# A fused attention, feed-forward and expert kernel: when the first feed-forward weights are loaded, and in which order the second head pair is prepared

## The chip, the cores and the metric

The kernel runs on one core of a Trainium2 chip. The metric is the device time of one launch in microseconds, lower is better. The kernel before takes 721.33 us (median of three runs, 720.0 to 721.43).

## The reference

Three stages follow each other. Shapes are fixed; all arrays are float32.

```python
# 1 attention within clusters: batch 2, heads 8, seq 768, head_dim 64, 16 clusters per head
q_assign = argmax(q_n @ c_n.T); k_assign = argmax(k_n @ c_n.T)      # normalised rows and centroids
mask   = q_assign[:, :, :, None] == k_assign[:, :, None, :]
scores = where(mask, q @ k.T / sqrt(64), -1e9)
attn   = exp(scores - max) / (sum + 1e-9)
x      = (attn @ v) -> (1536, 512)
# 2 feed-forward: w_in (512, 2048), w_out (2048, 512)
h = x @ w_in;  g = max(h, 0) + alpha * min(h, 0);  x = g @ w_out
# 3 experts: 8 of them, top 1, for tokens with x @ w_skip > 0
e = argmax(x @ w_gate);  x[t] += gate * (relu(x[t] @ w1[e]) @ w2[e])
```

Only stage 1 is touched, together with the conversion of the first three blocks of stage 2's weights, which is spread over stage 1.

## The kernel before

Stage 1 works on eight head pairs, n = 0 to 7. A pair has 12 steps: k = 0 to 5 are the six row tiles of its first head, k = 6 to 11 those of the second, so that step i = 12 n + k. The order of the work is written out by hand: the loop of `attention` runs over the steps, and every engine gets its instructions in the order in which the loop calls the helpers. Nothing is rescheduled afterwards.

**A step.** `scores` (S) multiplies a tile of AB by AB (L305) and adds CD by CD (L308) into a PSUM tile s; DVE takes the row maximum (`highest`, L321), ACT the exponential (`expo`, L328). Two steps later PE transposes it (`transp`, L339), ACT copies the halves to eth (L341) and DVE takes the remainder etl (L342); a group of three steps is then multiplied by v (`pv`). There are two tiles s, so scores of step i+2 wait for `expo` of step i.

**The next pair, m = n + 1, is prepared while pair n runs.** Tp holds its transposed q and k (`load`). `scaleq` scales q on POOL (L225). `sims` multiplies Tp by the centroids on PE (L188, after steps k = 1 and 2), DVE finds maxima, and POOL weighs them (`weigh`, L201). `sims2` makes the one-hot cluster rows oh (on POOL L216, L217). `split` writes RL: the rounded parts of q and k (part 0, L233, four instructions) and their remainders (part 1, L238, four). `onehots` turns oh on PE (L252, tile po), and ACT copies it to st (L263, L264). `place` copies RL into AB and CD of one head (three DMAs, L283 to L285, 384 KB each), `placeoh` copies st into the last rows of CD (three DMAs, L290, 32 KB each). RL has one buffer: the next pair's `split` waits until all `place` copies of this pair have read it. There is one AB and one CD for each of the two heads; the second head's copies are issued at k = 0 of the pair itself.

**At the end of a head pair** POOL also widens the reciprocal sums (`recip`, rx, L388), which PE transposes (`recip2`, pb, L397), and normalises the output of the pair before (L409 to L412, eight instructions of about 1 us).

**The feed-forward weights** come as raw 64-bit words. `Convert.load` fetches a block f (two DMAs of 512 KB, L551 and L552); `steps` converts it in four quarters of four slots each: two instructions on ACT (L579, L580), then one on DVE in each of three slots (L582, L584, L586), and one on POOL (L588) in the slot that opens the next quarter. A slot is used at steps i from CV0 on, except at k in CVX = (5, 6, 7, 8, 11). After a block the block f + 2 is loaded and REST slots stay empty.

**DMAs.** All those named are issued by SP, in program order. Each completion has one of eight semaphores in turn, and an issue waits until the DMA eight before it has landed.

Of the kernel before, what the change touches and what calls it, by code (L numbers as in the profile page):

```python
# [84 lines left out]
XG = (1, 6)  # L85
HT = 4
PACE = 7.5
CV0 = 12
LK = 8
XB = 3  # L90
LATE = 3
# [1 line left out]
PREP = (33, 45)  # L93
OK = 8
CVX = (5, 6, 7, 8, 11)
REST = 4
SIM, SP, S2, VS = (1, 2), (2, 3), 3, (8, 10)
ORD = ("SMAPXaBbE", "SMAPaVBXEb", "SAPXBMabE")

# [1 line left out]
def attention(ctx, tc, A, cst, xs, Tp, conv=None, prepare=None, then=None):  # L101
# [101 lines left out]
    def sims2(n, xs=(0, 1)):  # L203
        eq = pairs[n]
        if xs[0] == 0:
            hots[n] = hk.tile([P, 2, NT, 32], BF16, tag="oh", name="oh", bufs=1)
        g = G // 2
        gs = slice(xs[0] * g, (xs[-1] + 1) * g)
        m2 = wk.tile([P, G], F32, tag="m2", name="m2")
        nc.vector.tensor_reduce(out=m2[:, gs], in_=eq[:, gs], axis=AX.X, op=ALU.max)  # L210
        oh, mb = hots[n].rearrange("p x t (j c) -> p (x t j) c", c=NC_)[:, gs], m2[:, gs].unsqueeze(2).to_broadcast([P, gs.stop - gs.start, NC_])
        if n == 0:
            nc.vector.tensor_tensor(out=oh, in0=eq[:, gs], in1=mb, op=ALU.is_equal)
        else:

            nc.gpsimd.tensor_tensor(out=eq[:, gs], in0=eq[:, gs], in1=mb, op=ALU.subtract)  # L216
            nc.gpsimd.tensor_scalar(out=oh, in0=eq[:, gs], scalar1=-1.0, scalar2=1.0, op0=ALU.max, op1=ALU.add)  # L217
# [9 lines left out]
    def split(n, part):  # L227
        if part == 0:
            RL = wk.tile([P, 4, S], F32R, tag="RL", name="RL", bufs=1)
            heads[n] = RL  # L230
            for x in range(2):
                for u in halves:
                    nc.gpsimd.tensor_tensor(out=RL[:, 1 + x, u], in0=Tp[:, x, u], in1=zero.to_broadcast([P, S // 2]), op=ALU.add)  # L233
        else:
            RL = heads[n]
            for x in range(2):
                for u in halves:
                    nc.gpsimd.tensor_tensor(out=RL[:, 3 * x, u], in0=Tp[:, x, u], in1=RL[:, 1 + x, u].bitcast(F32), op=ALU.subtract)  # L238
# [10 lines left out]
    def turn(oh, po, x):  # L249

        for g in range(2):
            nc.tensor.matmul(po[:96, (2 * x + g) * P:(2 * x + g + 1) * P], lhsT=oh[:, x, 3 * g:3 * g + 3].rearrange("p t c -> p (t c)"),  # L252
                             rhs=identb, start=True, stop=True)

    def onehots(n):
        oh = hots.pop(n)
        po = ps_t.tile([P, 512], F32, tag="pt", name="po")
        for x in range(2):
            turn(oh, po, x)
        pv = po.rearrange("p (x g s) -> p x g s", x=2, g=2)  # L260
        st = hk.tile([96, 2, 2, P], F32R, tag="st", name="st", bufs=1)
        heads[n, "st"] = st
        nc.scalar.copy(st[:, 0], pv[:96, 0])  # L263
        nc.scalar.activation(st[:, 1], pv[:96, 1], AF.Copy, bias=-BIG, scale=BIG)  # L264
# [22 lines left out]
    def placeoh(n, j):  # L287
        o = slice(D + j * NC_, D + (j + 1) * NC_)
        for t in range(3):
            nc.sync.dma_start(out=CDs[j][o].bitcast(F32).rearrange("p x (g t s) -> p x g t s", g=2, t=3)[:, :, :, t],  # L290
                              in_=heads[n, "st"][32 * t + j * NC_:32 * t + (j + 1) * NC_].bitcast(F32))
# [6 lines left out]
    def scores(i):  # L298
        hd, t = divmod(i, NT)
        n, j = divmod(hd, 2)  # L300
        AB, CD = ABs[j], CDs[j]
        s = ps_s.tile([P, 2, 512], F32, tag="s", name="s")
        for u in range(2):
            ks = slice(u * 384, (u + 1) * 384)
            nc.tensor.matmul(s[:, u, :384], lhsT=AB[:, 0, t * P:(t + 1) * P], rhs=AB[:, 1, ks], start=True, stop=False)  # L305
        for u in range(2):
            ks = slice(u * 384, (u + 1) * 384)
            nc.tensor.matmul(s[:, u, :384], lhsT=CD[:, 0, t * P:(t + 1) * P], rhs=CD[:, 1, ks], start=False, stop=True)  # L308
        if t % 3 == 0:
            if j == 0:  # L310
                dens[n, t // 3] = wk.tile([P, 2, 3], F32, tag="den", name="den", bufs=4)
            den = dens[n, t // 3][:, j]
            eth = wk.tile([P, NT, 384], F32R, tag="eth", name="eth", bufs=2)
            etl = wk.tile([P, NT, 384], F32R, tag="etl", name="etl", bufs=2)
            grp[i // 3] = (den, eth, etl)
        es[i] = s
# [65 lines left out]
    def recip(n, g):  # L382
        rd = wk.tile([P, 2, 3], F32, tag="rd", name="rd")
        nc.vector.tensor_scalar(out=rd, in0=dens[n, g], scalar1=1e-9, scalar2=None, op0=ALU.add)
        nc.vector.reciprocal(out=rd, in_=rd)
        rx = wk.tile([P, 3, 2, D], F32, tag="rx", name="rx", bufs=1)
        eng = nc.gpsimd if n < len(seq) - 1 else nc.vector
        eng.tensor_copy(rx.rearrange("p t j d -> p j t d"), rd.unsqueeze(3).to_broadcast([P, 2, 3, D]))  # L388
        dens[n, g] = rx
# [55 lines left out]
    def before():  # L445
        for f in range(3):
            yield from conv.steps(f, 4)
            if f < 2:
                conv.load(f + 2)
                for _ in range(REST):  # L450
                    yield
# [3 lines left out]
    for i in range(NI + L + 7):  # L455
        n, k = divmod(i, 12)
        m = n + 1
        if i == NI and then is not None:
            early.close()
            for _ in first:  # L460
                pass
            fill = then()
            next(fill)
        if conv is not None and i in (2, 3):
            conv.load(i - 2)
        if conv is not None and i == PREP[0]:
            nc.sync.dma_start(out=al, in_=A["alpha"].rearrange("(f p) -> f p", p=P))
        if conv is not None and i == PREP[1]:
            pa = ps_t.tile([P, 512], F32, tag="pt", name="pa")
            nc.tensor.transpose(pa[:, :DFF // P], al, ident[:DFF // P, :DFF // P])  # L470
            prepare(pa[:, :DFF // P])
        if i % 3 == 1 and 0 <= i - 4 < NI and (i - 4) // 3 % 4 > 1:
            recip((i - 4) // 12, (i - 4) // 3 % 2)
        gi, part = divmod(i - L - 3, 3)
        live = 0 <= gi < NI // 3
        back = 0 <= i - L < NI
        for do in ORD[i % 3]:
            if do == "S" and i < NI:
                scores(i)
            if do == "S" and k == 0 and n < len(seq):  # L480
                place(n, 1)
                placeoh(n, 1)
            if do == "M" and i < NI:
                highest(i)
            if do == "P" and live:
                pv(gi, part)
                if part == 1 and gi % 4 > 1:
                    recip2(gi // 4, gi % 2)
            if do in "AB" and back:
                transp(i - L, "AB".index(do))  # L490
            if do in "ab" and back:
                lows["ab".index(do)]()
            if do == "V" and live:
                evac(gi)
            if do == "E" and i < NI:
                expo(i)
            if do == "X" and conv is not None and CV0 <= i and (k not in CVX or i >= NI - 12):

                next(first, None)
        if live and part == 2 and gi % 4 > 1:  # L500
            late.append((i + (LATE if i < NI else 0), gi))
        if late and late[0][0] <= i:
            gl = late.pop(0)[1]
            spare += normalize(gl // 4, gl % 2)
            while spare and i < NI:
                spare.pop(0)()
        for _ in range(FILL[max(i - NI, 0)] if i >= NI else 0):
            next(fill, None)
            if spare and i > NI + NRM:
                spare.pop(0)()  # L510
        if m < len(seq):
            if k in SIM:
                sims(m, SIM.index(k))
            if k == S2 and m == 1:
                sims2(m)
            if k in SP:
                split(m, SP.index(k))
            if k == S2 and m > 1:
                sims2(m)
            if k == 6:  # L520
                place(m, 0)
            if k == (OK if m > 1 else OK - 1):
                onehots(m)
                placeoh(m, 0)
            if k == LK and m + 1 < len(seq):
                load(m + 1)
            if k == VS[0]:
                vsplit(m, 0)
            if k == VS[1]:
                vsplit(m, 1)  # L530
            if k == 11 and m + 1 < len(seq):
                scaleq(m + 1)
# [1287 lines left out]
```

## Time and profile before

| | |
|---|---|
| median of 3 runs | 721.33 us |
| the profiled execution: time, span of the profile | 721.68 us, 719.9 us |
| PE, DVE, ACT, POOL busy, of the span | 97%, 79%, 66%, 53% |
| chain that ended last: PE, DMA, DVE, POOL, ACT | 67%, 9%, 6%, 6%, 5% |
| TensorE clock granted, mean | 0.994 |

The profiled execution is 0.35 us above the median. The span holds everything between the first and the last instruction; 1.8 us lie around it. Busy time of PE is that of pipelined matmuls, whose ends are modelled, so that short gaps of PE are read from the starts of its instructions. Stage 1 lies between about 13 us and 250 us.

### The profile page before, as it was taken

How to read it: one execution, taken by the hardware profiler on the slowest of the kernel's cores; microseconds unless marked ns; L12 is line 12 of the kernel's file. 1: busy time of each engine (PE TensorE's matmuls, PEld its weight loads, DVE VectorE, ACT ScalarE, POOL GpSimd, SP SyncE). 2: the span in 40 equal slices, each digit the busy share in tenths (PEclk: the TensorE clock that was granted, in tenths of full speed). 3: DMA queues.
4: the chain of work that ended last, by engine and by line, in shares of the span. 5: the costliest groups of instructions: out<-in, count | busy, mean ns of one | idle time of the engine just before them, and what ended most of it. 6: DMA issues, size and time to landing. Idle time of an engine off the chain costs nothing.

```text
span 719.9 us, 11791 instructions
## 1 busy us (share of the span) xinstructions
PE 701.3 (97%) x4119; PEld 627.2 (87%) x4119; DVE 566.4 (79%) x1112; ACT 471.9 (66%) x904; POOL 382.3 (53%) x339
## 2 busy tenths in 40 slices
PE   8999999999999999999999999999999999999995
PEld 5989999989998899888889999999888989898884
DVE  5888998799989878888884989977468888786651
ACT  5779798888889964445544655556645867574640
POOL 4539797697976486666662000001025888884201
PEclk9999999999999999999999999999999999999998
DMA  7885678656775133334303600016443998997000
GB/s 208 212 198 128 148 171 180 160 138 140 169 179 104 61 117 117 117 127 136 132 16 117 192 0 1 1 59 198 151 150 130 385 381 312 346 348 268 33 10 25
DMA packets 44128, 109.21 MB, mean 152 GB/s; under 512 B 8730, under 2 KB 24554, under 8 KB 38688
## 3 DMA queue, kind: packets, MB, share of 16 engines
q1 hardware_dynamic: 36992, 67.81, 34.6%
q0 software_dynamic: 7072, 40.60, 15.2%
q8 instruction: 34, 0.56, 0.3%
q14 instruction: 30, 0.25, 0.1%
HBM read 74.78 MB, written 10.10 MB: 118 GB/s over the span
## 4 chain that ended last, share of the span: by engine, by line
PE 67%; DMA 9%; DVE 6%; POOL 6%; ACT 5%; issue 4%; SPq 1%; POOLq 0%; ACTq 0%; DVEq 0%
PE h L671 18%; PE y L720 15%; DMA raw<-in_wall_dram,wi 6%; PE yo L1204 5%; PE pt L339 4%; PE hw L1257 4%; PE h L1204 3%; PE s L305 2%; PE px L357 2%; PE s L308 2%; PE y L730 2%; ACT e L328 2%; PE sim L188 2%; PE px L359 2%; DVE etl L342 2%
## 5 line engine op out<-in xcount | busy, mean ns | idle before, releaser
L342 DVE TENSOR_TENSOR etl<-pt,eth 128x384 fp32r<-128x384 f32 x192 | 102.1, 549 | 20.4 <-ACT eth L341 19.1
L341 ACT CAST eth<-pt 128x384 fp32r<-128x384 f32 x192 | 91.1, 486 | 21.7 <-PE pt L339 21.7
L1171 POOL DMA_INDIRECT xg<-y1d,gi x16 | 27.6, 1727 | 130.1 <-DVE gi L1020 113.8
L339 PE MATMUL pt<-ident,e 128*128 128x128 f32 x576 | 94.5, 274 | 0.3 <-ACT e L328 0.3
L321 DVE TENSOR_REDUCE nm<-s 128x1 f32<-128x768 f32 x96 | 90.4, 943 | 3.9 <-PE s L308 3.7
L328 ACT ACTIVATE e<-s,nm 128x768 f32<-128x768 f32 x96 | 87.4, 911 | 4.2 <-DVE nm L321 3.3
L699 ACT CAST gh<-gm 128x384 fp32r<-128x384 f32 x60 | 30.9, 514 | 81.7 <-DVE gm L697 58.5
L339 PEld LDWEIGHTS pt<-ident,e 128*128 128x128 f32 x576 | 74.2, 141 | 7.1 <-ACT e L328 0.6
L701 DVE TENSOR_TENSOR gl<-gm,gh 128x384 fp32r<-128x384 f32 x60 | 49.4, 823 | 25.7 <-ACT gh L699 25.7
L357 PE MATMUL px<-etl,vh 128*64 128x384 f32 (+1 forms) x192 | 65.4, 368 | 1.4 <-DVE etl L342 1.1
L305 PE MATMUL s<-AB 128*128 128x384 f32 x192 | 57.6, 381 | 2.3 <-ACT e L328 2.0
L571 POOL TENSOR_TENSOR pre<-ct,pre 128x512 int32<-128x512 int32 x26 | 37.2, 1452 | 35.8 <-DVE ct L569 35.8
L671 PE MATMUL h<-xh,wh 128*128 128x384 f32 x256 | 55.6, 338 | 0.6 <-DVE gm L694 0.4
L671 PE MATMUL h<-xh,wl 128*128 128x384 f32 x256 | 56.0, 339 | 0.0
L671 PE MATMUL h<-xl,wh 128*128 128x384 f32 x256 | 55.0, 336 | 0.0
L1539 DVE TENSOR_TENSOR wl<-raw,wh 128x2048 fp32r<-128x2048 f32 (+2 forms) x26 | 44.4, 1713 | 12.3 <-ACT wh L1535 11.0
L359 PE MATMUL px<-eth,vh 128*128 128x384 f32 x160 | 54.0, 337 | 0.0
L308 PE MATMUL s<-CD 128*128 128x384 f32 x192 | 49.7, 340 | 1.5 <-DMA CD<-st 1.0
L671 PEld LDWEIGHTS h<-xh,wh 128*128 128x128 f32 x256 | 45.5, 188 | 3.3 <-DVE gm L694 0.5
L671 PEld LDWEIGHTS h<-xh,wl 128*128 128x128 f32 x256 | 44.6, 188 | 2.7 <-POOL wl L643 2.6
L671 PEld LDWEIGHTS h<-xl,wh 128*128 128x128 f32 x256 | 45.7, 188 | 0.0
L1535 ACT CAST wh<-raw 128x2048 fp32r<-128x2048 f32 (+2 forms) x26 | 37.3, 1443 | 11.2 <-PE yo L1204 11.2
(352 smaller groups left out, 1815.3 us busy)
## 6 DMA issues: line engine op xcount, KB each, us to landing
AB<-RL SPq DMA_DIRECT2D x32, 384.0 KB, 5.2
raw<-in_w_in_dram SPq DMA_DIRECT2D x16, 512.0 KB, 4.0
raw<-in_w_out_dram SPq DMA_DIRECT2D x16, 512.0 KB, 4.7
raw<-in_wall_dram SPq DMA_DIRECT2D x8, 1024.0 KB, 7.4
Tp<-in_qkT_dram SPq DMA_DIRECT2D x16, 384.0 KB, 3.7
CD<-RL SPq DMA_DIRECT2D x16, 384.0 KB, 6.8
raw<-in_wall_dram POOLq DMA_DIRECT2D x4, 1024.0 KB
vt<-in_v_dram SPq DMA_DIRECT2D x8, 384.0 KB, 6.2
```

The lines of the kernel that those rows point to most:

```text
L305: nc.tensor.matmul(s[:, u, :384], lhsT=AB[:, 0, t * P:(t + 1) * P], rhs=AB[:, 1, ks], start=True, stop=False)
L308: nc.tensor.matmul(s[:, u, :384], lhsT=CD[:, 0, t * P:(t + 1) * P], rhs=CD[:, 1, ks], start=False, stop=True)
L321: nc.vector.tensor_reduce(out=nm, in_=s[:, :, :384], axis=AX.XY, op=ALU.max, negate=True)
L328: nc.scalar.activation(e.rearrange("p (u c) -> p u c", u=2), s[:, :, :384], AF.Exp, bias=nm, accum_out=den[:, i % 3:i % 3 + 1])
L339: nc.tensor.transpose(pt[:, i2], e[:, kt * P:(kt + 1) * P], ident)
L341: nc.scalar.copy(eh, pt)
L342: lows[u] = lambda: nc.vector.tensor_tensor(out=etl[:, 3 * u:3 * u + 3, q * P:(q + 1) * P], in0=pt, in1=eh.bitcast(F32), op=ALU.subtract)
L357: nc.tensor.matmul(px[:m], lhsT=vh[:, kt, :m], rhs=etl[:, kt], start=False, stop=False)
L359: nc.tensor.matmul(px, lhsT=vh[:, kt, :], rhs=eth[:, kt], start=False, stop=(kt == NT - 1))
L671: nc.tensor.matmul(hs[c], lhsT=a[:, k * P:(k + 1) * P], rhs=x[:, k, c * HC:(c + 1) * HC], start=(k == 0 and i == 0), stop=(k == KD - 1 and ...
L720: nc.tensor.matmul(ys[gi * GT + t], lhsT=a[:, t * P:(t + 1) * P], rhs=w, start=(f == 0 and n == 0), stop=(gi == 0 and f == NF - 1 and n == 2))
L1204: nc.tensor.matmul(out, lhsT=l[:, k], rhs=r[:, k * DM:(k + 1) * DM], start=start and k == 0 and i == 0, stop=stop and k == 3 and i == len( ...
```

## The change

Three things are moved; no instruction is added or removed.

- The raw blocks 0 and 1 are loaded at steps 9 and 21 instead of 2 and 3 (RAW).
- The conversion's first slot is step 16 instead of 12 (CV0), and two slots instead of four stay empty after a block (REST).
- For the second pair (m = 1) both parts of `split` follow `sims2` at k = 3, where part 0 stood ahead of it at k = 2; and `onehots` with `placeoh` follows step 6 and stands ahead of `place`, where it followed step 7 and stood behind `place`.

```diff
+RAW = (9, 21)
-CV0 = 12
+CV0 = 16
-REST = 4
+REST = 2
...
-        if conv is not None and i in (2, 3):
-            conv.load(i - 2)
+        if conv is not None and i in RAW:
+            conv.load(RAW.index(i))
...
             if k == S2 and m == 1:
                 sims2(m)
-            if k in SP:
+                split(m, 0)
+                split(m, 1)
+            if k in SP and m > 1:
                 split(m, SP.index(k))
             if k == S2 and m > 1:
                 sims2(m)
+            if k == (OK if m > 1 else 6):
+                onehots(m)
+                placeoh(m, 0)
             if k == 6:
                 place(m, 0)
-            if k == (OK if m > 1 else OK - 1):
-                onehots(m)
-                placeoh(m, 0)
```

SP's queue, from the raw loads to the copies for the second head of the second pair, before (AB0, CD0: first head, AB1, CD1: second head):

```order
L551 DMA raw0_78<-in_w_in_dram 128x4x256
L552 DMA raw0_78<-in_w_out_dram 128x1024
L283 DMA AB0_165<-RL_341 64x1536
L285 DMA CD0_166<-RL_341 64x2x768
L290 DMA CD0_166<-st_492 16x4x128 x3
L130 DMA Tp_91<-in_qkT_dram 128x768 x2
L132 DMA vt_526<-in_v_dram 128x2x384
L283 DMA AB1_167<-RL_341 64x1536
L285 DMA CD1_168<-RL_341 64x2x768
```

The same stretch of SP's queue now (line numbers are 1 to 3 higher in the changed file):

```order
L291 DMA CD0_166<-st_456 16x4x128 x3
L284 DMA AB0_165<-RL_368 64x1536
L286 DMA CD0_166<-RL_368 64x2x768
L131 DMA Tp_91<-in_qkT_dram 128x768 x2
L133 DMA vt_522<-in_v_dram 128x2x384
L554 DMA raw0_78<-in_w_in_dram 128x4x256
L555 DMA raw0_78<-in_w_out_dram 128x1024
L284 DMA AB1_167<-RL_368 64x1536
L286 DMA CD1_168<-RL_368 64x2x768
```

The one-hot copies now lead the RL copies of the first head, and the raw load of block 0 stands between the third pair's loads and the copies for the second head. Block 1 takes the same place one pair later.

POOL's queue in the second pair's preparation, before:

```order
L233 TENSOR_TENSOR RL<-Tp,zero 128x384 x4
L216 TENSOR_TENSOR eq<-eq,m_373 128x384
L217 TENSOR_SCALAR oh<-eq 128x384
L238 TENSOR_TENSOR RL<-Tp,RL 128x384 x4
L246 TENSOR_TENSOR vh<-vt,vh 128x6x64
```

And now:

```order
L217 TENSOR_TENSOR eq<-eq,m_364 128x384
L218 TENSOR_SCALAR oh<-eq 128x384
L234 TENSOR_TENSOR RL<-Tp,zero 128x384 x4
L239 TENSOR_TENSOR RL<-Tp,RL 128x384 x4
L247 TENSOR_TENSOR vh<-vt,vh 128x6x64
```

The one-hots moved ahead of the four casts. One pair later, POOL's queue behind the one-hots of the third pair was before:

```order
L217 TENSOR_SCALAR oh<-eq 128x384
L588 TENSOR_TENSOR w32a<-raw_78,w32a 128x256
L409 TENSOR_TENSOR xa<-xa,xb 128x384
L410 TENSOR_TENSOR xa<-xa,rb 128x384
L411 TENSOR_TENSOR xh_86<-xa,zero 128x384
```

And is now:

```order
L218 TENSOR_SCALAR oh<-eq 128x384
L410 TENSOR_TENSOR xa<-xa,xb 128x384
L411 TENSOR_TENSOR xa<-xa,rb 128x384
L412 TENSOR_TENSOR xh_86<-xa,zero 128x384
L413 TENSOR_TENSOR xl_87<-xa,xh_86 128x384
```

The conversion's L588 (L591 in the changed file) left this place, since the conversion opens a quarter later.

## Rows read from the trace of the kernel before

**Rows 1.** Windows, third pair: stretch, us, busy time and count by engine, clock, DMA.

```profile
73.86:103.50 29.64, 29.11 (x206) 27.25 (x204) 26.65 (x51) 26.13 (x63) 25.06 (x28) 1.00 0.65 147
```

**Rows 2.** Timeline of PE: start us, us, engine, line, op, tiles, idle before and releaser.

```profile
42.12 0.59 PE L308 MATMUL s<-CD 128*128 128x384 f32 x2 [0.99 <-DMA CD<-st]
...
64.48 0.39 PE L252 MATMUL po<-identb,oh 128*96 128x128 bf16 x4
...
72.77 0.34 PE L359 MATMUL px<-eth,vh 128*128 128x384 f32 x1
73.23 0.55 PE L397 MATMUL pb<-ident,rx 128*128 128x128 f32 x3
```

**Rows 3.** Timeline of SP's queue: first the copies of pair 1's first head.

```profile
29.37 0.52 SPq L283 DMA_DIRECT2D AB<-RL  x1
...
35.69 0.59 SPq L285 DMA_DIRECT2D CD<-RL  x1
...
37.03 3.44 SPq L290 DMA_DIRECT2D CD<-st  x3
...
44.10 1.91 SPq L285 DMA_DIRECT2D CD<-RL  x1
```

**Rows 4.** Line L283, the issue at 29.37: us from issue to landing.

```profile
DMA to landing us min/median/max: 3.8/3.8/3.8
```

**Rows 5.** Line L285, the issue at 44.10: us from issue to landing.

```profile
DMA to landing us min/median/max: 8.9/8.9/8.9
```

**Rows 6.** Line L290, three issues from 66.6 on: duration ns; us to landing.

```profile
L290 SPq DMA_DIRECT2D CD<-st x3: 586/622/637, 66.6 to 68.0; - x3
...
DMA to landing us min/median/max: 2.0/2.0/2.0
```

**Rows 7.** Line L551, raw loads issued at 21.39 and 23.74: us to landing.

```profile
DMA to landing us min/median/max: 6.0/6.3/6.5
```

**Rows 8.** Line L552, raw loads issued at 22.02 and 24.21: us to landing.

```profile
DMA to landing us min/median/max: 6.8/7.1/7.3
```

**Rows 9.** Timeline of ACT around steps 6 and 7 of the first pair.

```profile
30.63 0.91 ACT L328 ACTIVATE e<-s,nm 128x768 f32<-128x768 f32 x1
...
32.73 0.92 ACT L328 ACTIVATE e<-s,nm 128x768 f32<-128x768 f32 x1
...
33.87 0.40 ACT L264 ACTIVATE st<-po 96x256 fp32r<-96x256 f32 x1
```

**Rows 10.** Timeline of POOL, from the second pair's preparation on.

```profile
26.16 3.18 POOL L233 TENSOR_TENSOR RL<-Tp,zero 128x384 fp32r<-128x384 f32 x4 [1.74 <-DMA CD<-st]
...
31.75 3.92 POOL L238 TENSOR_TENSOR RL<-Tp,RL 128x384 fp32r<-128x384 f32 x4
...
52.21 1.01 POOL L201 TENSOR_TENSOR eq<-eq,cw 128x384 f32<-128x384 f32 x1 [4.90 <-DMA CD<-st]
53.17 3.37 POOL L233 TENSOR_TENSOR RL<-Tp,zero 128x384 fp32r<-128x384 f32 x4
...
61.31 1.50 POOL L217 TENSOR_SCALAR oh<-eq 128x384 bf16<-128x384 f32 x1
62.79 0.75 POOL L588 TENSOR_TENSOR w32a<-raw,w32a 128x256 int32<-128x256 int32 x1
...
72.67 0.50 POOL L388 COPY rx<-rd 128x384 f32<-128x384 f32 x1
```

**Rows 11.** Waits of PE from 73 to 225 us: us in total, times, longest.

```profile
PE s L305 <- ACT e L328: 1.7, 5, 0.5
PE px L357 <- DVE etl L342: 0.8, 2, 0.6
```

**Rows 12.** Timeline of POOL, the same casts one pair later and in pair 4.

```profile
82.74 3.23 POOL L233 TENSOR_TENSOR RL<-Tp,zero 128x384 fp32r<-128x384 f32 x4
...
141.91 3.19 POOL L233 TENSOR_TENSOR RL<-Tp,zero 128x384 fp32r<-128x384 f32 x4
```

**Rows 13.** Line L285, the issue at 72.20 (second head of pair 2): us to landing.

```profile
DMA to landing us min/median/max: 9.0/9.0/9.0
```

## The prediction, on record before the result was known

> **What bounds the kernel now.** I read the page first: PE is busy for 97% of the span, so only gaps of PE count in stage 1. Next the windows: a pair of heads takes 29.64 us, of which PE shows 29.11 us, and the other engines 25 to 27 us each [rows 1]. Little can be won, but POOL, at 25.06 us, has hardly more room than PE, and what it does in a pair is one chain. Then PE's rows at the second pair: it idles 0.99 us at the first scores, at 42.12, until the last copy of st into CD has landed, and about 0.3 us at 73.23, where the transpose of rx comes 0.46 us behind the matmul at 72.77, while such matmuls there follow each other at 0.17 [rows 2]. The second gap is POOL's: from 52.21 on it has no idle time before the rx of 72.67 [rows 10]. From 73 us to 225 us PE waits 1.7 us for exponentials and 0.8 us for etl [rows 11]; what the spacing of the conversion costs is in these.
>
> **Part 1, the one-hots first.** Their price is counted from the copies into AB and CD that step 12 needs. POOL's idle 1.74 us at 26.16 lets the one-hots run ahead of the casts; the work is the same, so the remainders L238 end no later than before, at 31.75 + 3.92 = 35.67 us [rows 10]. St is made one step earlier: it ended at 33.87 + 0.40 = 34.27, and the exponentials ahead of it stand at 30.63 and 32.73, so it is ready near 32.2 [rows 9]. ACT still does the same in these steps, and PE's two transposes change places with a step of equal work: nothing. The three issues take 0.6 us each and land in 2.0 us when the queue is empty [rows 6], so they are done near 34.3, and only then come the RL copies, which had begun at 29.37 [rows 3]. One alone takes 3.8 us [rows 4]; against 2.0 us for the small ones that leaves about 1.8 us of transfer for 384 KB. The three therefore land near 34.3 + 3.8 = 38.1, 39.9 and 41.7 us. Before, the last landing was just short of 42.12 [rows 2], near 41.9. So the wait of 0.99 us doesn't go: its cause passes from the small copies to the large ones, and I count 0.2 us gained. Bounds: 1.0 us gained (the wait gone) to 1.0 us lost (each copy 0.3 us slower and the transfers of the next pair, issued right behind, in their way).
>
> The Trainium skill (DMA: Bandwidth & Descriptors, Anatomy of one DMA) gives 2.0 us fixed and the bytes at 436 GB/s, fitted to the other issue path. By it a 384 KB copy would take 2.9 us, the three would land by about 38.5, and the wait would be gone. The 3.8 us row speaks against that, since it was alone in the queue.
>
> **Part 2, block 0 loaded at step 9.** Before, the raw loads landed at 21.39 + 6.0 = 27.4, 28.8, 30.3 and 24.21 + 7.3 = 31.5 us [rows 7, 8], while SP had nothing else to copy until 29.37 [rows 3]; the first RL copy landed in its lone 3.8 us [rows 4]. They cost nothing there, so moving them gains nothing there. A block holds the queue for two of these intervals, 2 x (31.5 - 27.4) / 3 = 2.7 us. At step 9 it stands behind the next pair's loads and in front of the copies for the second head. Their last one landed at 44.10 + 8.9 = 53.0 us [rows 3, 5], and POOL's casts for the third pair, which overwrite the RL that it reads, began at 53.17, just as POOL was free of L201 [rows 10]. That was a cover of 0.2 us. Now the copy lands near 53.0 - 0.2 + 2.7 = 55.5, and the casts start near 55.6, 2.4 us late. Scores of the second head have time to spare; POOL has not. The one-hots of the third pair end at 61.31 + 1.50 + 2.4 = 65.2, and PE wants to turn them at 64.48 [rows 2, 10]: 0.7 us of the delay shows there. The conversion's L588 of 0.75 us at 62.79 has left this stretch, so rx is 2.4 - 0.75 = 1.65 us late, and so is the transpose at 73.23, which already waited for it. Pair 1 loses 1.65 us in all. Bounds: 0.3 us gained (loads that don't hold up the copies, and L588 gone) to 3.2 us lost (a block that takes 4.2 us, half as long again as these).
>
> **Part 3, block 1 at step 21.** Its copy landed at 72.20 + 9.0 = 81.2, and the casts began at 82.74 behind L201 [rows 12, 13]: 1.5 us of cover. PE and L201 are 1.65 us later now, while the copies, which follow the one-hots, are only 0.7 us later plus 2.7 for the block, at 84.6. The casts would start at 82.74 + 1.65 = 84.4. Cost 0.2 us, counted as nothing; without the cover it would be 2.7 us.
>
> **Part 4, the conversion.** Up to step 37 the slots have the same kind of work in both, for the shift of four steps is one quarter; the last quarter of block 0 falls on steps 38 to 45, which were empty. Block 1 follows with fewer empty slots. The two ACT instructions that open a quarter move from steps 12, 46, 51, 60, 64 to 38, 49, 57, 62, 70. Steps k = 0 to 2 have room on ACT, since PE does sims there; at the others they delay an exponential, which PE sees two steps later. Of such places three go (46, 51, 64) and two come (57, 70). Of the waits of 1.7 and 0.8 us at most half hangs on these, and POOL, which now has an L588 more in pair 3, gives part of it back. I take 0.5 us gained; bounds 2.5 us gained (all of these waits) and 0.75 us lost (that L588 alone, shown in full).
>
> **The sum.** -0.2 + 1.65 - 0.5 = +0.95 us. On the profiled execution's 721.68 us, of which 719.9 us are the span, that is 722.6; the profiled execution stood 0.35 us above the median of the runs, so the median comes to 722.3 us. What a measurement can tell from no change is 0.2%, 1.4 us either side of 721.33, so this counts as no change, near its upper edge.
>
> **Rival A, slower: POOL is the bound and nothing is given back.** Place: the casts of every pair before which a block is loaded, pairs 2 and 5 first. The load of block 2 falls to step 46 now, again just ahead of a second head's copies; in pair 4 the casts at 141.91 stand behind L201 [rows 12]. If POOL's chain, and not PE, sets each pair, the 0.5 us of part 4 is not earned, the L588 of 0.75 us in pair 3 shows in full, and the block at step 46 shows with what exceeds a cover like that of pair 2, 2.7 - 1.5 = 1.2 us: -0.2 + 1.65 + 0.75 + 1.2 = +3.4, or 724.7 us. It decides from the point where rx of a later pair is behind PE again. For it: POOL's 25 us of each 30 in one chain with DMA waits. Against it: PE's waits behind 73 us name ACT and DVE, not POOL [rows 11].
>
> **Rival B, faster: the block doesn't hold up the copies.** If loads from HBM and copies inside SBUF pass each other, the casts start at 53.2 as before, L588's leaving removes the 0.3 us at 73.23, and the wait at 42.12 may shrink by half, 0.5 us. With 1.0 us from part 4 that is -1.8 us, 719.5. For it: they don't read from the same memory. Against it: the copy issued at 44.10, behind loads from HBM and other copies, took 8.9 us where a lone one takes 3.8 [rows 4, 5], so a queue is what they stand in.
>
> The Trainium skill (DMA: Bandwidth & Descriptors, Queues, rings and completion order) says that completion is not in the order of issue for one issuing engine. By that rule the copies could land ahead of the block, and the time would be rival B's. The rows on the raw loads, which land at 27.4, 28.8, 30.3 and 31.5 in the order of their issue, don't bear it out.
>
> **Rival C: the first wait goes.** The large copies land by 40.8 and PE's 0.99 us vanishes, the rest as in the sum: -1.0 + 1.65 - 0.5, about +0.15, 721.5 us. It is inside no change too.
>
> **Chances.** Forecast 0.40, A 0.30, B 0.22, C 0.08. Faster by over 0.2%: B, 0.22. Slower by over 0.2%: A, and the upper tail of the forecast (more than 0.5 us above its sum), 0.30 + 0.04 = 0.34. Within: 0.44. The forecast's own range is 721.0 to 723.6; the 8-in-10 range reaches into both rivals, 719.6 to 724.4.
>
> **What would show it.** Right: in the profile after, PE still idles about 0.7 to 1.2 us before the first L308 of the second pair, now released by the copy CD<-RL; the third pair's casts start about 2.4 us later against L201's end and are released by that copy; PE waits near its turn of the one-hots and before the rx transpose. Wrong: casts right behind L201 (then B), no wait at the second pair's first scores (then C), or rx waits again in pairs 3 to 5 (then A). A first stretch to the second pair's start that is longer or shorter by more than 1 us would mean that the order of ACT's work in steps 6 to 8 was not free.

## The result, and the profile after

The changed kernel takes 726.28 us (median of 5 runs, 725.77 to 729.34) against 721.43 us before (5 runs); the ratio on record is 1.0085, with a 95% interval of 1.0070 to 1.0099. (Here and below the ratio is the record's own estimate; it is not the quotient of the two medians, which is 1.0067 here. All ratios are against the kernel before.) It is slower, by 4.9 us in the medians, and lies outside the range of 719.6 to 724.4. The profiled execution after took 726.28 us, 4.6 us more than that of before. The page after begins:

```profile
span 724.5 us, 11791 instructions
...
PE 702.1 (97%) x4119; PEld 627.4 (87%) x4119; DVE 568.9 (79%) x1112; ACT 472.1 (65%) x904; POOL 383.5 (53%) x339
```

PE's busy time is 0.8 us more than before, the span 4.6 us more, so most of the difference is idle time. Most line numbers are 1 to 3 higher after (L308 is L309, L233 is L234). First the timeline of PE at the second pair's first scores, which answers to [rows 2]:

```profile
41.45 0.76 PE L309 MATMUL s<-CD 128*128 128x384 f32 x2 [1.87 <-DMA CD<-RL]
```

The wait has grown from 0.99 to 1.87 us. Its releaser is the large copy, as forecast; its length was forecast at 0.7 to 1.2 us. Behind it the granted clock is low (1.00 is 2.4 GHz, 0.50 is 1.2 GHz; a value between them is a stretch with some of each). Windows of PE after (stretch, us, busy and count, granted clock, DMA share, GB/s):

```profile
7.00:12.00 5.00, 4.73 (x25) 0.66 0.87 176
17.00:23.00 6.00, 6.00 (x49) 1.00 1.00 224
40.00:46.00 6.00, 4.55 (x21) 0.72 0.95 308
```

The same three windows of before:

```profile
7.00:12.00 5.00, 3.97 (x28) 1.00 0.88 177
17.00:23.00 6.00, 6.00 (x38) 0.72 1.03 234
40.00:46.00 6.00, 5.01 (x35) 1.00 0.79 244
```

A clock of 0.72 over 6 us is 6 x 0.28 = 1.7 us of full speed lost. In this execution of before one such stretch lay at 17 to 23 us; after, it lies at 7 to 12, where PE waits in any case, and a second one follows the longer wait. So PE comes to step 12 earlier in the trace of after than in that of before, and times of the two traces near this place are compared by their distances. First before, then after:

```profile
40.54 0.60 PE L305 MATMUL s<-AB 128*128 128x384 f32 x2
```

```profile
38.99 0.59 PE L306 MATMUL s<-AB 128*128 128x384 f32 x2
```

These are 1.55 us apart. At the last step of stage 1 PE is 4.55 us later than before, so the change costs 6.1 us from step 12 on; the difference of the two profiles, 4.6 us, is smaller by what the low stretch had cost before.

Next the waits of PE from 75 to 225 us (us in total, times, longest), which answer to [rows 11]:

```profile
PE pb L398 <- POOL rx L389: 3.6, 2, 1.8
PE po L253 <- POOL oh L218: 1.9, 2, 1.0
PE px L358 <- DVE etl L343: 0.7, 1, 0.7
PE s L306 <- ACT e L329: 0.5, 1, 0.5
```

5.5 us of waits for POOL are new, twice a pair of waits for one-hots and rx: once in pair 2, once in pair 4, as the windows of 80 to 110 and 140 to 170 us show. The wait for exponentials has shrunk from 1.7 to 0.5 us. Where POOL's lateness comes from stands in its timeline (the casts of [rows 12]):

```profile
82.60 1.02 POOL L202 TENSOR_TENSOR eq<-eq,cw 128x384 f32<-128x384 f32 x1 [4.00 <-DVE eq L195]
86.19 3.37 POOL L234 TENSOR_TENSOR RL<-Tp,zero 128x384 fp32r<-128x384 f32 x4 [2.57 <-DMA CD<-st]
...
147.68 3.36 POOL L234 TENSOR_TENSOR RL<-Tp,zero 128x384 fp32r<-128x384 f32 x4 [2.45 <-DMA CD<-st]
```

And the chain of waits from 80 to 104 us (start, us, what), which begins with the copies and ends at PE:

```profile
74.61 11.57 DMA CD<-st
...
86.19 3.37 POOL RL L234 x4
89.56 3.89 POOL RL L239 x4
93.44 0.80 POOL eq L217
...
94.33 1.51 POOL oh L218
...
95.89 0.42 PE po L253 x4
```

A late copy delays the casts, and POOL has no idle time between them and the one-hots that PE turns. (The profile names the small copy CD<-st, which landed last before the casts, at 86.17; RL, which the casts overwrite, is read by CD<-RL, and that landed at 85.94.) What made the copies late is seen in SP's queue at step 9:

```profile
39.91 0.43 SPq L133 DMA_DIRECT2D vt<-in_v_dram  x1
40.39 0.47 SPq L554 DMA_DIRECT2D raw<-in_w_in_dram  x1
40.90 0.50 SPq L555 DMA_DIRECT2D raw<-in_w_out_dram  x1
...
43.38 0.69 SPq L286 DMA_DIRECT2D CD<-RL  x1
```

The view of DMA issues of that stretch gives KB each and us from issue to landing:

```profile
raw<-in_w_in_dram SPq DMA_DIRECT2D x1, 512.0 KB, 6.5
raw<-in_w_out_dram SPq DMA_DIRECT2D x1, 512.0 KB, 8.2
vt<-in_v_dram SPq DMA_DIRECT2D x1, 384.0 KB, 5.1
CD<-RL SPq DMA_DIRECT2D x1, 384.0 KB, 11.5
```

So v lands at 39.91 + 5.1 = 45.0, the block's halves at 46.9 and 49.1, and the last large copy at 54.9. The block takes 49.1 - 45.0 = 4.1 us; the copies behind it take 5.8, and the same passage took 5.7 before. I call the time from v's landing to that of CD<-RL the passage:

| kernel | passages without a raw block between, us | with one, us |
|---|---|---|
| before | 5.2 to 5.9 (6 pairs) | none |
| after | 5.1 to 5.6 | 9.8, 10.6, 9.6 |
| the second pair's old order (below) | 5.2 to 5.7 | 10.7, 10.4, 10.3 |
| the conversion alone (below) | 4.9 to 6.2 | 11.1 |
| one more block in front (below) | 5.2 to 6.4 | 9.7 |

### The profile page after: what moved, and what is told of

Read it like the earlier page. It is cut to its first block, busy times and chain, and to the rows that moved or that the text cites. A ratio compares the mean times of both kernels' runs of the same rounds, so it can differ in the third digit from the quotient of the medians.

```text
span 724.5 us, 11791 instructions
## 1 busy us (share of the span) xinstructions
PE 702.1 (97%) x4119; PEld 627.4 (87%) x4119; DVE 568.9 (79%) x1112; ACT 472.1 (65%) x904; POOL 383.5 (53%) x339
## 4 chain that ended last, share of the span: by engine, by line
PE 65%; DMA 11%; DVE 7%; ACT 6%; POOL 5%; issue 4%; SPq 1%; POOLq 0%; ACTq 0%; DVEq 0%
PE h L674 18%; PE y L723 15%; DMA raw<-in_wall_dram,wi 6%; PE yo L1207 6%; PE hw L1260 4%; PE pt L340 3%; PE h L1207 3%; DMA CD<-st 3%; DMA CD<-RL 2%; PE y L733 2%; PE px L358 2%; PE s L306 2%; PE s L309 2%; ACT e L329 2%; DVE etl L343 2%
## 5 line engine op out<-in xcount | busy, mean ns | idle before, releaser
L306 PE MATMUL s<-AB 128*128 128x384 f32 x192 | 57.5, 380 | 1.1 <-ACT e L329 0.7
L309 PE MATMUL s<-CD 128*128 128x384 f32 x192 | 49.5, 338 | 1.9 <-DMA CD<-RL 1.9
```

## The experiments

The theory was that the loss comes of raw blocks that stand in SP's queue in front of the second head's copies and so hold up POOL's casts, with the longer first wait beside it. Rival R1: the second pair's new order makes it. Rival R2: the conversion's new spacing makes it.

**Raw blocks 0 and 1 early again.**

```diff
-RAW = (9, 21)
+RAW = (2, 3)
```

> The kernel after with the raw blocks 0 and 1 loaded at steps 2 and 3 again, the rest of the change kept. Theory (a raw block in SP's queue in front of the copies for the second head holds POOL's casts up): the casts of the third pair stand right behind L202 again, the lag of the scores that grew from 0.9 us at step 24 to 3.3 us at step 37 in the kernel after is gone, block 2 at step 46 still costs about 2 us between steps 57 and 61; 722.9 us, between 722.0 and 724.0. Rival R1 (the order of the second pair, with its longer first wait and the low clock behind it, makes the loss): still 725 us or more. Rival R2 (the new spacing of the conversion on ACT and POOL makes it): 724.5 us or more.

Measured: 725.39 us, ratio 1.0066 (1.0052 to 1.0080); the profiled execution 723.84. Its waits of PE from 75 to 225 us:

```profile
PE pb L398 <- POOL rx L389: 1.8, 1, 1.8
PE po L253 <- POOL oh L218: 1.6, 1, 1.6
```

One pair of waits is gone, that of pair 2; that of pair 4, where block 2 still stands in front, is left. That is the theory's picture, and the profiled time is in its interval, but the median is not: by time alone R1's number was met, and the ratio's interval overlaps that of the kernel after. The other runs had to decide.

**The second pair's old order.** In the kernel after:

```diff
-                split(m, 0)
-                split(m, 1)
-            if k in SP and m > 1:
+            if k in SP:
...
-            if k == (OK if m > 1 else 6):
-                onehots(m)
-                placeoh(m, 0)
             if k == 6:
                 place(m, 0)
+            if k == (OK if m > 1 else OK - 1):
+                onehots(m)
+                placeoh(m, 0)
```

> The kernel after with the old order of the second pair (one-hots behind the casts), the loads at steps 9 and 21 and the conversion from step 16 kept. Theory: only the longer first wait goes, 0.9 us, and pair 2 still waits for its casts; 725.4 us, between 724.5 and 726.3. R1 (the second pair's order): 722.5 us or less. R2 (the conversion): about 725.5 us, as the theory.

Measured: 727.29 us, ratio 1.0091 (1.0078 to 1.0105). R1 is out, and the theory missed too: nothing was gained. The timeline of POOL shows why:

```profile
55.79 3.18 POOL L234 TENSOR_TENSOR RL<-Tp,zero 128x384 fp32r<-128x384 f32 x4 [4.71 <-DMA CD<-st]
...
85.46 3.18 POOL L234 TENSOR_TENSOR RL<-Tp,zero 128x384 fp32r<-128x384 f32 x4 [0.29 <-DMA CD<-st]
```

And its waits of PE from 40 to 75 us:

```profile
PE po L253 <- POOL oh L218: 2.4, 1, 2.4
PE s L309 <- DMA CD<-st: 1.0, 2, 0.8
```

Without the longer first wait PE is in time, and block 0 shows in pair 1: the casts wait 4.71 us, PE 2.4 us, and the granted clock is 0.68 from 64 to 68 us. Then PE is late, and block 1 finds a cover: 0.29 us. In the kernel after it is the other way round. What delays PE first hides what comes next.

**The conversion's spacing alone**, in the kernel before:

```diff
-CV0 = 12
+CV0 = 16
...
-REST = 4
+REST = 2
```

> The kernel before with the conversion from step 16 and two slots between blocks, nothing else. Theory: the spacing gives 1.4 us back in steps 48 to 60, and block 2, now issued at step 46 in front of the fifth pair's second-head copies, takes about 2 us at its casts; 722.0 us, between 721.0 and 723.2. R1: 720 us, the gain alone. R2: 724 us or more.

Measured: 722.52 us, ratio 1.0024 (1.0012 to 1.0035). Its waits of PE from 75 to 225 us:

```profile
PE po L252 <- POOL oh L217: 2.4, 1, 2.4
PE pb L397 <- POOL rx L388: 1.8, 1, 1.8
PE s L305 <- ACT e L328: 0.9, 2, 0.5
```

Both effects are there: the exponentials' wait falls from 1.7 to 0.9 us, and block 2, now issued at step 46 in front of the copies, costs 4.2 us of waits. The clock does not fall behind them, though 2.4 us is more than the first wait of the kernel after. The window behind that wait:

```profile
154.53:160.00 5.47, 5.47 (x40) 1.00 0.51 115
```

**The second pair's new order alone**, in the kernel before: the lines of the change to `split`, `onehots` and `placeoh`, without the rest.

> The kernel before with the second pair's new order alone (one-hots ahead of the casts and placed first). Theory: the first scores of the second pair wait about 0.9 us longer in all, some of which the wait of the rx transpose behind it takes up; 722.0 us, between 721.2 and 722.8. R1: 724.5 us or more, most of the 4.85 us lost. R2: 721.3 us.

Measured: 723.55 us, ratio 1.0026 (1.0014 to 1.0038): more than the theory's 722.0, less than R1's. The wait is 1.88 us (`CD<-RL`), as in the kernel after, and no wait for POOL is among PE's later ones. What the theory left out is, by the trace, the low clock, 0.55 from 44 to 46 us and 0.60 from 46 to 48.

**Block 2 behind the copies.** The kernel before with the conversion's new spacing, and the load one slot later, at step 48:

```diff
             if f < 2:
+                yield
                 conv.load(f + 2)
-                for _ in range(REST):
+                for _ in range(REST - 1):
                     yield
```

> The kernel before with the conversion from step 16, two slots between blocks, and block 2 issued at step 48 again, behind the copies for the fifth pair's second head. Theory (a block in front of second-head copies makes PE wait twice, for the one-hots and for rx): the two waits of 2.4 and 1.8 us that the conversion alone has in pair 4 go, the shorter waits for exponentials stay; 720.0 us, between 719.0 and 721.2. Rival (the spacing of the conversion itself, more ACT and POOL work in pair 4, makes those waits): 722.5 us, as with the conversion alone.

Measured: 720.38 us, ratio 0.9982 (0.9971 to 0.9992), 2.1 us less in the medians than with the load at step 46, 0.42% less by the ratios, whose intervals lie apart. Its waits of PE from 75 to 225 us are for ACT and DVE again:

```profile
PE s L305 <- ACT e L328: 1.4, 3, 0.5
PE px L357 <- DVE etl L342: 0.7, 1, 0.7
```

The spacing is a gain, and one slot of one load had turned it into a loss. This version beats both kernels.

**One more block in front, and the same one behind.** The kernel before loads block 1 a second time, at step 21, and the other kernel at step 25; the bytes are the same:

```diff
+        if conv is not None and i == 21:
+            conv.load(1)
```

> The kernel before with one more load of block 1 at step 21, the same bytes a second time, in front of the third pair's second-head copies; nothing else is changed. Theory: the block takes some 4 us of SP's queue, 1.5 us of which is cover, so POOL's casts wait some 2.5 us and PE waits for the one-hots and for rx, 2.8 to 4.2 us together: 724.7 us, between 723.8 and 725.6. By the price of 2.7 us for a block that the prediction used: 722.5 us. Rival (the loss is not the queue's but comes of the conversion or of the second pair): 721.3 us.

> The kernel before with one more load of block 1 at step 25, the same bytes a second time, behind the third pair's second-head copies; nothing else is changed. Theory (only the place in SP's queue counts, not the bytes): no wait of PE for one-hots or rx in pair 2, 721.4 us, between 720.6 and 722.2. Rival (the extra bytes on the DMA engines cost the time wherever they are issued): 723 us or more, as with the block at step 21.

Measured in front: 723.58 us, ratio 1.0034 (1.0021 to 1.0046); behind: 721.22 us, ratio 1.0001 (0.9988 to 1.0014). In front, POOL's casts and PE's waits from 75 to 225 us are:

```profile
84.35 3.36 POOL L233 TENSOR_TENSOR RL<-Tp,zero 128x384 fp32r<-128x384 f32 x4 [2.30 <-DMA CD<-st]
```

```profile
PE pb L397 <- POOL rx L388: 1.8, 1, 1.8
...
PE po L252 <- POOL oh L217: 0.9, 1, 0.9
```

Behind, there is no wait for POOL at all:

```profile
PE s L305 <- ACT e L328: 1.5, 4, 0.5
PE px L357 <- DVE etl L342: 0.6, 1, 0.6
```

A megabyte more costs nothing behind the copies and about 2.4 us in front of them (0.2 us less than the theory's interval allowed). The price per block of the prediction, 722.5 us, is too small, and R1 and R2 can't explain this pair, since neither kernel has their parts.

**The first wait filled.** To the second pair's new order alone, twelve matmuls of a zero tile are added in front of step 12's scores:

```diff
+        for x in range(12 if i == 12 else 0):
+            nc.tensor.matmul(s[:, x % 2, :384], lhsT=warm[:, :P], rhs=warm[:, :384], start=True, stop=True)
```

> The kernel before with the second pair's new order, and twelve matmuls of a zero tile put ahead of the first scores of the second pair, where PE idles 1.9 us. Theory (the stretch of granted clock 0.5 behind that idle time belongs to it and costs 1.4 us): the clock stays at 1.00 there and the time is 722.1 us, between 721.5 and 722.8. Rival (the low stretch has nothing to do with the idle time, as in the kernel before, where it comes at 18 us): 723.5 us, or more, as with the second pair's order alone.

Measured: 722.21 us, ratio 1.0018 (1.0004 to 1.0032). The window of 40 to 46 us:

```profile
40.00:46.00 6.00, 6.00 (x41) 1.00 1.00 276
```

The clock stays at full speed there, and the median is 1.3 us lower than without the filling, as expected; by the ratios it is only 0.08% lower, and their intervals overlap, so the trace carries this and the time does not. In that profile PE then waits 1.0 us for rx at the end of the pair, which didn't show without the filling, where PE was later.

**The raw blocks on ACT's queue.** In the kernel after, blocks 0 to 2 are issued by ACT, at the same steps:

```diff
-        self.nc.sync.dma_start(out=raw[:, :DM].rearrange("p (k n) w -> p k (n w)", k=DM // P), in_=self.w_in[:, :, f])
-        self.nc.sync.dma_start(out=raw[:, DM:].rearrange("p n w -> p (n w)"), in_=self.w_out[:, f])
+        q = self.nc.scalar if f < 3 else self.nc.sync
+        q.dma_start(out=raw[:, :DM].rearrange("p (k n) w -> p k (n w)", k=DM // P), in_=self.w_in[:, :, f])
+        q.dma_start(out=raw[:, DM:].rearrange("p n w -> p (n w)"), in_=self.w_out[:, f])
```

> The kernel after with the raw blocks 0 to 2 issued by ACT instead of SP, at the same steps, so that they do not stand in SP's queue. Theory (the place in SP's queue is what counts): the casts of the pairs 2 and 4 follow L202 without a wait and PE's waits for one-hots and rx go; the longer first wait stays and the conversion's gain too; 722.0 us, between 721.0 and 723.4. Rival (what counts is the share of the 16 DMA engines and of the memory, whoever issues): 725 us or more, with waits of 1 us or more before the casts.

Measured: 729.60 us, ratio 1.0109 (1.0093 to 1.0125). A miss: the rival's time was met, and in pair 4 its wait too. POOL's casts of pairs 1 and 2 do follow L202 without a wait (57.86 behind 56.89, 87.20 behind 86.23), and the passages there are 6.1 and 4.7 us. But they don't show that a block on another queue lets the copies pass, for ACT issued these blocks earlier against SP's queue, and both had landed before v: at 47.2 against 48.5 us, and at 75.5 against 81.2. Only in pair 4 is the block under way together with the copies. KB each and us from issue to landing there (the issues stand at 133.04, 136.14, 132.99 and 135.57 us):

```profile
raw<-in_w_in_dram ACTq DMA_DIRECT2D x1, 512.0 KB, 15.4
raw<-in_w_out_dram ACTq DMA_DIRECT2D x1, 512.0 KB, 13.9
vt<-in_v_dram SPq DMA_DIRECT2D x1, 384.0 KB, 7.9
CD<-RL SPq DMA_DIRECT2D x1, 384.0 KB, 14.4
```

The halves and the last copy landed at 148.4, 150.0 and 150.0 us, the passage was 9.2 us, and the casts waited 1.41 us. That is the rival's picture: another queue did not help the copies where the block ran beside them. So what holds the copies up, as far as these cases show, is a block that is transferred ahead of them or along with them; on one queue its place decides which it is. Most of the time was lost elsewhere, for ACT stood still (its timeline at step 9):

```profile
34.70 3.92 ACTq L555 DMA_DIRECT2D raw<-in_w_in_dram  x1
...
38.66 1.78 ACTq L556 DMA_DIRECT2D raw<-in_w_out_dram  x1
40.48 0.86 ACT L342 CAST eth<-pt 128x384 fp32r<-128x384 f32 x2 [4.58 <-issue]
```

The two issues took 5.7 us on ACT, and PE waited 3.7 us for the etl that follows that cast. At the later two places each issue took 0.34 to 0.52 us, but in pair 4 the second came 2.7 us after the end of the first, ACT was idle for 2.96 us, and PE waited 2.3 us for an exponential. The loss moved to an engine that has less room for it.

The Trainium skill (DMA: Bandwidth & Descriptors, Issuing engines are not separate DMA queues) says that DMAs of all engines run on the same 16 DMA engines and interleave, and that issuing on several only saves the sequencer's time. Pair 4, with its passage of 9.2 us, agrees with the interleaving; the 5.7 us on ACT in pair 1 are no saving, and the measurement decides.

**Every block behind the copies.** The kernel after with blocks 0, 1 and 2 at steps 13, 25 and 48:

```diff
-RAW = (9, 21)
+RAW = (13, 25)
```

and the slot of block 2 as above.

> The kernel after with every raw block behind the second-head copies of its pair: blocks 0, 1 and 2 at steps 13, 25 and 48. The second pair's new order and the conversion's new spacing stay. Theory: the casts' waits of pairs 2 and 4 go, what is left is the first wait with its low clock (2.3 us lost) and the conversion's gain (1.3 us): 722.3 us, between 721.5 and 723.3. Rival (late raw loads or the new order cost something of their own beside the first wait): 724.5 us or more.

Measured: 722.94 us, ratio 1.0019 (1.0002 to 1.0037). Its waits from 75 to 225 us name ACT and DVE only, and its first wait is there:

```profile
PE s L309 <- DMA CD<-RL: 2.1, 1, 2.1
```

With the new order and the new spacing both kept, the place of the three blocks alone makes 726.28 into 722.94 us. That is within the theory's interval, and it settles the question that the first run left open. Against the first run, where block 2 alone stood in front, it is 0.47% less (the intervals lie apart), and the step from 46 to 48 was worth 0.42% with the conversion alone: by these numbers block 2 is the largest single part of the loss, though not clear of block 1's 0.34%.

**The parts together.** Each alone on the kernel before: the new order +0.26%, block 1 in front +0.34%, the spacing with block 2 in front +0.24%. The sum is 0.84%, the change 0.85%; block 0 has no kernel of its own here and no term. That the two meet so closely is in part luck: each interval reaches 0.12% to either side, the medians of the three add up to 2.4 + 2.2 + 1.4 = 6.0 us against 4.9, and the first two experiments show that taking a part away does not give its price back. Where the kernel after loses is read from the starts of PE's scores (L306 after, L305 before): 2.25 us from step 12 to 14, the first wait and the low clock; 0.15 us in the rest of pair 1; 2.5 us from step 32 to 37, behind block 1; 0.6 us gained up to step 56; 2.0 us lost from there to step 63, behind block 2.

## Why the prediction was wrong, step by step

- **Part 1 was mis-sized: -0.2 us expected, about +2 us measured.** That the wait would pass to the large copies was right, and that the small ones land early too. But the three large copies landed at 36.5, 38.8 and 41.3 us, 2.3 to 2.5 apart, not the 1.8 that I took from one lone landing by a subtraction [rows 4, 6]. (These times are early against the forecast's because PE and all behind it ran 1.55 us earlier in this execution. Nor was that landing lone: it was issued at 29.37, and by [rows 8] the last raw load landed at 31.5.) The wait grew by 0.88 us, which the bound of 1.0 lost held. What no bound held is the low clock behind it: the order alone costs 0.26%, 1.9 us, and in its trace PE's scores fall back by 2.3 us from step 12 to 14, of which the longer wait is 0.9. The estimate that the prediction draws from the Trainium skill (DMA: Bandwidth & Descriptors, Anatomy of one DMA) should come to 34.3 + 2.9 + 0.9 + 0.9 = 39.0 us, not 38.5; nothing hangs on it.
- **Part 2, the price of a block: 2.7 us expected, 4.1 measured.** The mechanism (a queue in which the copies stand behind the block) was right, and my upper bound of 4.2 named the size in pair 1; in pairs 2 and 4 the passage grew by 5.3 and 3.7 us (10.6 against 5.2, 9.6 against 5.9). I took the interval of loads that had the queue nearly to themselves [rows 7, 8] for loads that stand between v and the copies; why they take longer there is not shown. The casts came at 55.00 instead of 55.6, since the loads ahead landed early in this execution (v at 45.0, before at 47.2), and 1.07 us behind L202's end instead of 2.4. Pair 1 then hardly lost by it: against before, PE's scores start 0.70 us later behind the first wait and 0.85 us later at the start of pair 2, so about 0.15 us instead of 1.65, since PE was late already; with the old order the same block cost 2.4 us there, and a low clock.
- **Part 3 is the step that failed, together with the block 2 that Part 4 left out: each counted a block in front of second-head copies as nothing.** "Cover 1.5 us, cost counted as nothing" needed a block of 2.7 us and a PE that is 1.65 us later. The copy landed at 85.9 us, not at 84.6, the casts began at 86.19, not at 84.4, and pair 2 paid 2.8 us. The kernel with that one block in front has the same pair of waits, 2.7 us, with nothing else changed.
- **Part 4: the gain was there, the move of block 2 was not counted, a term of 2 to 3 us.** The spacing gives 0.18% (1.3 us; 0.5 expected, bound 2.5). But the sum had the load at step 46 in Rival A alone; with a passage of 11.1 us it costs 2.1 us with the conversion alone (722.52 against 720.38; 0.42% by the ratios), and in the kernel after, with 9.6 us, 2.8 us of waits.
- **Rival A named the right engine and, with the casts at 141.91, the right place for block 2**, but not the whole mechanism: the gain of the spacing, which it denied, was earned. Its price for block 2 was 2.7 - 1.5 = 1.2 us, and it left pair 2 and the low clock at nothing; hence 724.7 and not 726.3. What I held against it, that PE's waits before name ACT and DVE [rows 11], says who is last now, not by how much POOL is ahead. POOL's room was the 1.5 us between the copy's landing and the casts [rows 12, 13], and that was the number to weigh.
- **Rivals B and C** didn't occur: on one queue the copies never passed the block, and the first wait stayed. What B's case against the queue left out is that a block can hold copies up from another queue as well, as pair 4 with the loads on ACT shows.

The rule of the Trainium skill (DMA: Bandwidth & Descriptors, Queues, rings and completion order), by which completion need not follow the order of issue for one issuing engine, showed in none of the passages here: with a block between, all were 9.6 us or longer. In every trace here, the landings of SP's transfers between 13 and 225 us stand in the order of issue.

What stays open: why the medians differ more from the profiled executions than the traces explain (the first experiment's profile is 1.6 us below its median). Open, too, is why one idle stretch of PE is followed by the low clock and another, as long or longer, is not. Each kernel has one trace, and the low stretch of the clock in the first 25 us lies elsewhere from one to the next, or is absent.

## What to carry to other kernels

Before a load is moved, look at what stands behind it in its queue, and what is transferred beside it, at the new place, and measure the cover of that: from the landing to the start of its reader. A load that is free at one place can cost 2 to 3 us at another, two steps away, and a version with the same parts and other slots can be faster than both. Price a transfer by its interval in company of the same kind, not alone, and when several delays are possible, sum them in order of time, for the first one hides part of the next.

## What the runs showed of the hardware

- A 1 MB block between other transfers of one queue lengthened their passage from 4.6 to 6.7 us (all traces) to 9.6 to 11.1 us (9 passages), though the four halves of two blocks in [rows 7, 8] landed 1.3 to 1.4 us apart. Issued on ACT's queue and in flight beside the copies, a block still made the passage 9.2 us (one case).
- PE's 1.9 us of idle time at the second pair was followed by a granted clock of 0.5 to 0.7 in the kernel after and with the new order alone; with matmuls of zeros in its place the clock stayed at 1.00. The idle 0.99 us of before had no such stretch behind it, but neither had 2.40 us of idle time in pair 4 with the conversion alone (1.00 from 154.53 to 160 us), so the length of the idle time does not decide alone.
- An issue of half a block took 0.5 us on SP in the rows of step 9 above, and 3.92 and 1.78 us on ACT at the same step of the program; the other four on ACT took 0.34 to 0.52 us. What made the first two long is not shown.
